# A decay factor fetched as one row and spread by matmuls, in place of a broadcast transfer

## The chip, the cores and the metric

The kernel runs on one core of a Trainium2 chip. The metric is the device time of one execution in microseconds (us); lower is better. A core has five engines with queues of their own: TensorE (PE, matmuls and, beside them, weight loads), VectorE (DVE), ScalarE (ACT), GpSimd (POOL) and SyncE (SP, which here only issues DMAs). ACT and POOL issue DMAs too. Each engine executes its queue in the written order, and a waiting instruction holds those behind it.

## The reference

Two layers. The first is an attention with exponential decay, over 4 batches, 8 heads, 768 positions and 64 channels, in blocks of 64 positions with a running state; each head h has its own decay lam[h], a number between 0.97 and 0.99. The second multiplies each token's 512 values by w_in (512 x 2048), applies a piecewise quadratic activation, and multiplies by w_out (2048 x 512).

```python
Dmask = np.where(rel >= 0, lam[:, None, None] ** rel[None, :, :], 0.0)
lam_pow = lam[:, None, None] ** (pos[None, :, None] + 1)
lam_block = lam ** block
...
intra = np.einsum('bhic,bhjc->bhij', qb, kb) * Dmask[None]
intra = np.einsum('bhij,bhjd->bhid', intra, vb)
inter = np.einsum('bhid,bhde->bhie', qb * lam_pow[None], kv_state)
out[:, :, sl] = intra + inter
...
h = x @ w_in
mid = ~neg & ~pos
g = np.where(pos, h, np.where(neg, 0.0, (h + beta) ** 2 / (4.0 * beta)))
return (g @ w_out).astype(np.float32)
```

lam is an input of 8 float32 numbers, 32 bytes.

## The kernel before, in words

The decay between two positions i and j is lam to the power i - j. The kernel writes it as a product: q at position i is multiplied by lam to the i and k at position j by lam to the minus j, with positions counted from the middle of the sequence. These factors stand in tables, one value for each position (partition) and head. `tables` (L110) makes a pair of them: DVE multiplies the positions by ln lam (`arg`, L113), and ACT takes the exponential twice, `tk` for k (L115) and `tq` for q (L117). The pair `tke`/`tqe` (argument `arge`) serves the first four units of work, the pair `tkd`/`tqd` (`argd`) all others. For this every partition needs ln lam of all 8 heads: L93 fetches lam into all 128 partitions of `lam_b` by a DMA that ACT issues, and ACT takes the logarithm, `ln_lam` (L104).

The first 512 tokens are computed in four units, u = 0 to 3, each with 256 positions and 4 heads. A unit loads q, k and v (`x0f`, `x1f`, `x2f`, L302, three DMAs of 256 KB on SP's queue). `qs` (POOL) and `ks` (DVE, both L315) multiply by the tables, `vs` (L313) casts v. PE transposes qs and ks (L329); ACT, and for later units DVE, copy the result from PSUM to `qT` and `kT` (L336). PE then makes the scores (`ps`, L373), which DVE masks (`sc`, L381), the state update (`pu`, L349, copied by ACT to `ue`, L364), and the two output terms (`py`, L393 and L408), which ACT copies to `xT` (L419). The remaining tokens follow in chunks of 128. The second layer takes 512 tokens at a time: L606 multiplies by w_in, ACT and DVE apply the activation, L639 multiplies by w_out. Its weights come in pieces by DMAs on POOL's queue (L152, L153); the first waits for the third unit's k load.

The order on each engine is written out by a planner, `run_plan`: every operation has a guessed duration, its needs and a due time, and the planner simulates the engines and emits the instructions in the order that this gives. The plan begins at 5000 ns for the engines; what stands before (constants, lam, tables) is emitted first, in program order. Between PE's first operations the planner puts warm-up matmuls on a tile of zeros `zz` (`warm`, L272 to L275), 4 x 128 columns or 128 columns each, into one PSUM bank, `ph`. How many is decided by the nominal time `at`, which starts at the first number of `WARM`:

```python
        at, n1 = WARM[0], 0
        for t, _, x in sorted(out_seq, key=lambda p: p[:2]):
            if x.eng == "PE" and n1 < 2:
                while at < t - (200 if at < WARM[1] else WARM[2]):
                    one_ns = 58 if at > WARM[1] else 110
                    n = 4 if at + 4 * one_ns < t - 200 else 1
                    warm(n)
                    at += n * one_ns
```

PSUM tiles named `po` come from a pool of one buffer; the transposes of the first unit's ks write there.

Of the kernel before, what the change touches and what calls it, by code (L numbers as in the profile page):

```python
# [8 lines left out]
F32 = mybir.dt.float32  # L9
BF16 = mybir.dt.bfloat16  # L10
I32 = mybir.dt.int32
AX = mybir.AluOpType
AF = mybir.ActivationFunctionType
# [10 lines left out]
def kernel(  # L24
# [16 lines left out]
    nc = tc.nc  # L41
    B, H, S, D = q.shape
# [8 lines left out]
    MS = 512  # L51
# [7 lines left out]
    RW, NR = 2, 3  # L59
    XT, MG, NQT, NQK, NVS, NUB, RING = 6, 6, 4, 4, 5, 4, 3.5  # L60
    DBG = False
    OB = 8

    const = ctx.enter_context(tc.tile_pool(name="const", bufs=1))
# [10 lines left out]
    rp = ctx.enter_context(tc.tile_pool(name="rp", bufs=NR))  # L75
    op = ctx.enter_context(tc.tile_pool(name="op", bufs=OB))
    PS = bass.MemoryType.PSUM
    pp_h = ctx.enter_context(tc.tile_pool(name="pp_h", bufs=2, space=PS))
# [3 lines left out]
    pp_o = ctx.enter_context(tc.tile_pool(name="pp_o", bufs=1, space=PS))  # L82
# [6 lines left out]
    SYNC = mybir.DependencyInfo(mybir.DependencyClass.Sync, mybir.DependencyReason.DATA)  # L89

    nc.scalar.preload_act_table_set("natural_log_exp_and_others")
    lam_b = const.tile([128, H], F32)
    nc.scalar.dma_start(out=lam_b, in_=lam.partition_broadcast(128))  # L93


    NE = 4
# [3 lines left out]
    make_identity(nc, ident)  # L100
    zz = const.tile([128, MS], BF16)
    nc.vector.memset(zz, 0.0)
    ln_lam = const.tile([128, H], F32)
    nc.scalar.activation(out=ln_lam, in_=lam_b, func=AF.Ln)  # L104
    pos_e = const.tile([128, NE], F32)
    nc.vector.tensor_copy(pos_e, pos_ei.rearrange("p a b -> p (a b)"))
    one = const.tile([128, 1], F32)
    nc.vector.memset(one, 1.0)  # L108


    def tables(pos, n, name):
# [11 lines left out]
    for t, base in ((mask2, 0), (mask2b, 128)):  # L123
        nc.gpsimd.memset(t, 1.0)
        nc.gpsimd.affine_select(
            out=t, in_=t, compare_op=AX.is_ge, fill=0.0,
# [7 lines left out]
        out=causal, in_=causal, compare_op=AX.is_ge, fill=0.0,  # L134
# [34 lines left out]
    def add(key, eng, ns, fn, needs=(), due=None, extra=0, dma=0, perf=False, mode=("full", "full"), ring=1, slack=0, late=0):  # L169
        OPS[key] = Op(key, eng, ns, fn, list(needs), due, extra, dma, perf, mode, ring, slack)  # L170
        OPS[key].late = late
        ops.append(OPS[key])

    def run_plan(free):
# [42 lines left out]
        while len(out_seq) < len(ops):  # L217
# [33 lines left out]
            for u in users[x.key]:  # L251
                left[u.key] -= 1
                if left[u.key] == 0:
                    ready[u.eng].append(u)
# [8 lines that stand above are left out]
                at = t + x.ns  # L263
                n1 += x.key[0] == "l1"
            if DBG:
                print(f"{t / 1e3:9.3f} {min(x.due, 9e6) / 1e3:9.3f} {x.eng:5s} {x.ns:6.0f} {x.end / 1e3:9.3f} {x.key}")
            x.fn()

    WARM = (1400, 7500, 700)
    wbank = []  # L270

    def warm(n):  # L272
        if not wbank:
            wbank.append(pp_h.tile([128, MS], F32, name="ph", tag="ph"))
        nc.tensor.matmul(wbank[0][:, 0:128 * n], lhsT=zz[:, 0:128], rhs=zz[:, 0:128 * n], start=True, stop=True, skip_group_check=True)  # L275

    def mm(*cols):
        return sum(c / 2.4 + 3 for c in cols)

# [372 lines left out]
    def f_ylast(part):  # L652
        cs = slice(CUT, d_model) if part else slice(0, CUT)
        if part == 0:
            osb["last"] = op.tile([128, d_model], F32, name="osb", tag="osb")
        nc.scalar.copy(out=osb["last"][:, cs], in_=py_t["last", part][:, cs])

    def f_stlast(part):
        cs = slice(CUT, d_model) if part else slice(0, CUT)
        nc.sync.dma_start(out=out[n_tok - 128:n_tok, cs], in_=osb["last"][:, cs])  # L660

    def f_y(s, ms):
        osb[s, ms] = op.tile([128, d_model], F32, name="osb", tag="osb")
        nc.scalar.copy(out=osb[s, ms], in_=py_t[s, ms])  # L664

    def f_out(s, ms):
        m0 = s * MS + ms * 128
        if s == 0:

            for j in range(2):  # L670
                nc.gpsimd.dma_start(out=out[m0:m0 + 128, :].rearrange("(p j) n -> j p n", j=2)[j], in_=osb[s, ms][HD[j], :])
        elif s < NST - 1:
            nc.gpsimd.dma_start(out=out[m0:m0 + 128, :], in_=osb[s, ms])  # L673
        else:
            nc.sync.dma_start(out=out[m0:m0 + 128, :], in_=osb[s, ms])
# [160 lines left out]
    for n1, (_, s, i, p) in enumerate(l1_order):  # L836
        prev = bank[on_y[n1]]
        n = PARTS.get(s, 1)
# [18 lines left out]
    for n2, (_, s, ms, kg) in enumerate(l2_order):  # L857
        n = PARTS.get(s, 1)
# [5 lines left out]
        if y == NCH - 1:  # L864
            if kg == 0:
                for part, n in ((0, CUT), (1, d_model - CUT)):
# [3 lines left out]
                    add(("y", y + part), "ACT", 400 - 240 * part, lambda part=part: f_ylast(part),  # L870
                        [("last", part), ("y", y - 1 + part), ("st", y - OB)], extra=95)
                    add(("st", y + part), "SP", 550 if s else 1100, lambda part=part: f_stlast(part), [("y", y + part), ("st", y - 1 + part)], due=-1,
# [5 lines left out]
        if kg == 3:  # L878
            add(("y", y), "ACT", 490, lambda a=(s, ms): f_y(*a), [("l2", n2), ("y", y - 1), ("st", y - OB)], extra=95)
            add(("st", y), "POOL" if s < NST - 1 else "SP", 1600 if s == 0 else 800 if s < NST - 1 else 550, lambda a=(s, ms): f_out(*a),  # L880
# [34 lines left out]
```

## Time and profile before

| | us |
|---|---|
| median of 3 runs | 209.01 (208.78 to 209.41) |
| the profiled execution, whole | 210.35 |
| its span, first to last instruction | 208.6 |
| PE busy in the span | 201.6 |
| DVE busy | 140.0 |
| ACT busy | 120.4 |
| issue of lam's transfer (L93) | 0.83 |
| start of `ln_lam` (L104) | 4.94 |
| start of the first `qs` on POOL (L315) | 5.84 |
| PE's warm-up matmuls before the first transposes | 15, from 1.26 to 6.56 |

The profile is of one execution; times in it count from the span's start. Busy time of PE is the time in which matmuls are under way, not that at which it is at its peak. An engine's idle time is put down to whatever released it last. Instructions that issue a DMA stand as SPq, ACTq or POOLq, with the time that the issue took.

### The profile page before, as it was taken

Reading aid. Unit: us, or ns where it says so; the run is one execution under the profiler, and the core shown is the slowest. Engines: PE = TensorE matmul, PEld = TensorE weight load, DVE = VectorE, ACT = ScalarE, POOL = GpSimd, SP = SyncE. Lnnn points to the kernel's source line nnn. Section 1 sums busy time; section 2 is a strip of 40 time slices with the busy share of each in tenths; the row PEclk is TensorE's granted clock in tenths of the full one; section 3 lists DMA queues with packets and bytes.
Section 4 is the critical chain, followed back from the end, with each engine's and each line's share of the span. In section 5 each row is a group of like instructions: output and inputs, shape, how many; then the busy total and the mean of one; then the engine's idle time right before and its main releaser. Section 6 shows DMA issues by size and latency. Waiting matters only on the chain.

```text
span 208.6 us, 6389 instructions
## 1 busy us (share of the span) xinstructions
PE 201.6 (97%) x2754; PEld 137.1 (66%) x2754; DVE 140.0 (67%) x245; ACT 120.4 (58%) x225; POOL 72.8 (35%) x95
## 2 busy tenths in 40 slices
PE   7779999999999999999999999999999999999994
PEld 2457887446866876666766767667667666666643
DVE  0575697453898786998877989976866656354510
ACT  2564675225865767585675786575675565464421
POOL 5598200145255173763554354335511011010000
PEclk9996999999999999999999999999999999999999
DMA  4999999999999999999999999999822002011112
GB/s 106 296 246 177 201 202 199 234 214 179 173 232 211 196 235 222 212 246 228 173 199 280 170 257 219 205 177 213 147 50 104 3 5 98 0 50 53 50 50 101
DMA packets 95051, 34.49 MB, mean 165 GB/s; under 512 B 82352, under 2 KB 93360, under 8 KB 95024
## 3 DMA queue, kind: packets, MB, share of 16 engines
q1 hardware_dynamic: 88464, 24.65, 65.4%
q0 software_dynamic: 6416, 9.44, 21.2%
q8 instruction: 21, 0.34, 0.7%
q14 instruction: 6, 0.05, 0.1%
q10 hardware_dynamic: 144, 0.00, 0.0%
HBM read 27.27 MB, written 6.29 MB: 161 GB/s over the span
## 4 chain that ended last, share of the span: by engine, by line
PE 90%; SPq 4%; DMA 3%; ACT 1%; issue 1%; DVE 0%; ACTq 0%
PE ph L606 40%; PE py L639 39%; SPq L302 4%; DMA x1f<-in_k_dram 3%; PE py L649 2%; PE ps L500 1%; PE py L606 1%; PE ps L492 1%; PE pu L527 1%; PE po L527 1%; PE po L511 1%; PE py L408 1%; DVE ks L315 0%; PE pu L511 0%; PE py L393 0%
## 5 line engine op out<-in xcount | busy, mean ns | idle before, releaser
L606 PE MATMUL ph<-xT,w_in_sb 128*128 128x256 bf16 (+1 forms) x872 | 94.8, 258 | 0.0
L639 PE MATMUL py<-w_out_sb,gT 128*128 128x512 bf16 x368 | 91.1, 379 | 0.0
L614 ACT ACTIVATE r<-ph,one 128x512 bf16<-128x512 f32 x93 | 63.9, 687 | 46.5 <-PE ph L606 40.9
L606 PEld LDWEIGHTS <-w_in_sb 128*128 128x128 bf16 x896 | 76.7, 98 | 19.9 <-issue 0.2
L639 PEld LDWEIGHTS <-gT 128*128 128x128 bf16 x368 | 34.9, 98 | 28.4
L622 DVE TENSOR_SCALAR t<-r 128x1024 bf16<-128x1024 bf16 x48 | 24.9, 518 | 32.3 <-ACT r L614 32.1
L630 DVE TENSOR_TENSOR gT<-w,t 128x1024 bf16<-128x1024 bf16 x48 | 39.8, 830 | 1.4
L625 DVE TENSOR_TENSOR w<-r,t 128x1024 bf16<-128x1024 bf16 x48 | 36.9, 769 | 1.6
L453 POOL TENSOR_TENSOR kq<-x1f,tkd 128x512 bf16<-128x512 f32 x18 | 20.5, 1139 | 23.8 <-DMA x1f<-in_k_dram 21.7
L673 POOL DMA_DIRECT2D out_dram<-osb x16 | 9.1, 571 | 50.1 <-ACT osb L664 48.4
L453 POOL TENSOR_TENSOR kq<-x0f,tqd 128x512 bf16<-128x512 f32 x18 | 20.6, 1144 | 15.6 <-DMA x0f<-in_q_dram 15.4
L664 ACT COPY osb<-py 128x512 f32<-128x512 f32 x23 | 13.5, 587 | 12.1 <-PE py L639 11.4
L565 DVE TENSOR_TENSOR sd<-ps,diag 128x256 bf16<-128x256 f32 x36 | 13.5, 415 | 3.0 <-PE ps L500 3.0
L443 ACT CAST vs<-x2f 128x512 bf16<-128x512 f32 x20 | 12.3, 616 | 2.2 <-DMA x2f<-in_v_dram 2.2
L539 DVE TENSOR_TENSOR st<-st,ps 128x256 f32<-128x256 f32 x30 | 12.4, 414 | 0.5
L544 ACT CAST us<-st 128x512 bf16<-128x512 f32 (+1 forms) x18 | 10.5, 581 | 2.0 <-DVE st L539 1.8
L548 ACT CAST xT<-po 128x256 bf16<-128x256 f32 x18 | 6.8, 377 | 4.7 <-PE pu L511 4.1
L450 POOL TENSOR_TENSOR kq<-x0f,tqd 128x512 bf16<-128x512 f32 x2 | 2.1, 1040 | 20.1 <-DMA x0f<-in_q_dram 20.1
L548 ACT CAST xT<-pu 128x256 bf16<-128x256 f32 x18 | 6.7, 374 | 2.3 <-PE po L511 2.3
L527 PEld LDWEIGHTS <-vs 64*64 64x64 bf16 x288 | 3.7, 107 | 6.5 <-issue 5.9
L275 PE MATMUL ph<-zz 128*128 128x512 bf16 (+1 forms) x18 | 6.3, 510 | 1.3 <-DVE one L108 1.3
L381 DVE TENSOR_TENSOR sc<-ps,mask 128x512 bf16<-128x512 f32 x8 | 5.2, 681 | 2.4 <-PE ps L373 2.4
(89 smaller groups left out, 135.3 us busy)
## 6 DMA issues: line engine op xcount, KB each, us to landing
x0f<-in_q_dram SPq DMA_DIRECT2D x24, 256.0 KB, 5.6
x1f<-in_k_dram SPq DMA_DIRECT2D x24, 256.0 KB, 5.2
x2f<-in_v_dram SPq DMA_DIRECT2D x24, 256.0 KB, 5.5
out_dram<-osb POOLq DMA_DIRECT2D x16, 256.0 KB, 4.0
w_out_sb<-in_moe_w_out_dram POOLq DMA_DIRECT2D x4, 512.0 KB, 13.6
w_in_sb<-in_moe_w_in_dram POOLq DMA_DIRECT2D x3, 512.0 KB, 7.0
out_dram<-osb POOLq DMA_DIRECT2D x8, 128.0 KB, 4.4
out_dram<-osb SPq DMA_DIRECT2D x3, 256.0 KB, 2.0
```

The lines of the kernel that those rows point to most:

```text
L443: (nc.scalar.copy if eng is nc.scalar else eng.tensor_copy)(t, qkv_ld[c, x])
L453: eng.tensor_tensor(t.rearrange("p (i g) d -> p g i d", g=2), qkv_ld[c, x].rearrange(h4, g=2), tb.rearrange(h4, g=2), op=AX.mult)
L539: nc.vector.tensor_tensor(st[c][:, a], st[c][:, 0] if a else st[c - 1][:, 1], kv[c][a], op=AX.add)
L548: nc.scalar.copy(out=get_xT(s)[:, :, off:off + 64], in_=po_of(c, a))
L565: nc.vector.tensor_tensor(sc_sb[c][:, par], pst[c, par], _bc(diag, 1, HP), op=AX.mult)
L606: nc.tensor.matmul(ph[:, j * m:(j + 1) * m], lhsT=w_in_sb[:, ko, (ni + j) * 128:(ni + j + 1) * 128], rhs=xT[s][:, ko, part * m:(part + 1) ...
L614: nc.scalar.activation(out=r_t[grp][:, i, :], in_=ph_t[s, ni, part], func=AF.Relu, bias=one[:, 0:1])
L622: nc.vector.tensor_scalar(t_t[grp], r, 0.5, 1.0, op0=AX.mult, op1=AX.min)
L625: nc.vector.tensor_tensor(w_t[grp], r, t_t[grp], op=AX.subtract)
L630: nc.vector.tensor_tensor(gT[s][:, f - RW * n:f, part * m:(part + 1) * m], w_t[grp].rearrange("p a (b m) -> p (a b) m", m=m), t_t[grp].rea ...
L639: nc.tensor.matmul(py_t[s, ms], lhsT=gT[s][:, ko, ms * 128:(ms + 1) * 128], rhs=w_out_sb[:, ko, :], start=(ko == 0), stop=(ko == FO - 1))
L664: nc.scalar.copy(out=osb[s, ms], in_=py_t[s, ms])
```

## The change

lam is fetched into one partition (`lam_1`, 1 x 8 float32). Three bfloat16 numbers are split off it in turn, each the rounded rest of what the ones before left (three casts and two subtractions on DVE, on one partition), and each is multiplied on PE by a column of ones: a matmul with `ones` (1 x 128) as weights adds up the three parts in float32 on all 128 partitions of a PSUM tile `po`. ACT takes the logarithm from there. Five warm-up matmuls are emitted ahead of the three, and the planner's nominal time for warm-ups starts by 5 x 440 ns later. The definition of `warm` moves up unchanged.

```diff
+    WARM_LAM = 5
...
-    lam_b = const.tile([128, H], F32)
-    nc.scalar.dma_start(out=lam_b, in_=lam.partition_broadcast(128))
+    lam_1 = const.tile([1, H], F32)
+    nc.scalar.dma_start(out=lam_1, in_=lam.rearrange("(o h) -> o h", o=1))
...
-    ln_lam = const.tile([128, H], F32)
-    nc.scalar.activation(out=ln_lam, in_=lam_b, func=AF.Ln)
...
+    ones = const.tile([1, 128], BF16)
+    nc.vector.memset(ones, 1.0)
...
+    for _ in range(WARM_LAM):
+        warm(4)
+    lam_p = [const.tile([1, H], BF16, name=f"lam{i}") for i in range(3)]
+    lam_r = [const.tile([1, H], F32, name=f"lamr{i}") for i in range(2)]
+    lam_b = pp_o.tile([128, MS], F32, name="po", tag="po")[:, 0:H]
+    rest = lam_1
+    for i in range(3):
+        nc.vector.tensor_copy(lam_p[i], rest)
+        if i < 2:
+            nc.vector.tensor_tensor(lam_r[i], rest, lam_p[i], op=AX.subtract)
+            rest = lam_r[i]
+        nc.tensor.matmul(lam_b, lhsT=ones, rhs=lam_p[i], start=(i == 0), stop=(i == 2))
+    ln_lam = const.tile([128, H], F32)
+    nc.scalar.activation(out=ln_lam, in_=lam_b, func=AF.Ln)
...
-    WARM = (1400, 7500, 700)
+    WARM = (1400 + 440 * WARM_LAM, 7500, 700)
```

On PE's queue this puts three matmuls of 8 columns behind the first five warm-ups; the ten others, and all that follows on every engine, keep their order. On DVE the five small operations stand behind the constants and ahead of `arge`.

More of the change, by code (lines that the diff above doesn't have):

```diff
@@ L108, with warm @@
     nc.vector.memset(one, 1.0)
+    ones = const.tile([1, 128], BF16)
+    nc.vector.memset(ones, 1.0)
+    wbank = []
+    def warm(n):
+        if not wbank:
+            wbank.append(pp_h.tile([128, MS], F32, name="ph", tag="ph"))
+        nc.tensor.matmul(wbank[0][:, 0:128 * n], lhsT=zz[:, 0:128], rhs=zz[:, 0:128 * n], start=True, stop=True, skip_group_check=True)
+    for _ in range(WARM_LAM):
[12 more added lines that the diff above has]
+    nc.scalar.activation(out=ln_lam, in_=lam_b, func=AF.Ln)
     def tables(pos, n, name):
@@ L267, in run_plan @@
             x.fn()
-    WARM = (1400, 7500, 700)
[L270 to L275, printed above, removed]
+    WARM = (1400 + 440 * WARM_LAM, 7500, 700)
     def mm(*cols):
```

## The prediction

> **What bounds the kernel now.** I read the page's chain that ended last first: it tells who is worth speeding up.
>
> ```profile
> PE 201.6 (97%) x2754; PEld 137.1 (66%) x2754; DVE 140.0 (67%) x245; ACT 120.4 (58%) x225; POOL 72.8 (35%) x95
> PE 90%; SPq 4%; DMA 3%; ACT 1%; issue 1%; DVE 0%; ACTq 0%
> ```
>
> PE is nine tenths of the chain, so the body isn't touched by an edit to the start. What can move is the moment at which PE's own run begins. The chain in order of time, cut to the first 30 us, shows that moment:
>
> ```profile
> 2.98 1.86 SPq L302
> ...
> 9.33 5.27 DMA x1f<-in_k_dram
> 14.60 0.02 issue
> 14.62 1.01 DVE ks L315
> 15.63 0.05 issue
> 15.67 0.40 PE po L329 x4
> ```
>
> (Start, length.) Up to 14.6 us the chain is the twelve loads of the first four units on SP's queue; the eleventh, k of the last unit, releases DVE, and from 15.67 it is PE. No lam stands in it. Where lam stands, the timelines of ACT, POOL and DVE say (start, length, in brackets the idle time before and its releaser):
>
> ```profile
> 0.83 0.42 ACTq L93 DMA_DIRECT2D lam_b<-in_lam_dram  x1
> 4.94 0.21 ACT L104 ACTIVATE ln_lam<-lam_b 128x8 f32<-128x8 f32 x1 [2.86 <-DMA lam_b<-in_lam_dram]
> 5.84 1.04 POOL L315 TENSOR_TENSOR qs<-x0f,tqe 128x512 bf16<-128x512 f32 x1 [1.60 <-ACT tqe L117]
> 6.67 0.76 DVE L315 TENSOR_TENSOR ks<-x1f,tke 128x512 bf16<-128x512 f32 x1 [0.97 <-DMA x1f<-in_k_dram]
> 9.01 0.69 DVE L381 TENSOR_TENSOR sc<-ps,mask 128x512 bf16<-128x512 f32 x1 [1.58 <-PE ps L373]
> 11.99 0.73 DVE L315 TENSOR_TENSOR ks<-x1f,tke 128x512 bf16<-128x512 f32 x1 [0.76 <-DMA x1f<-in_k_dram]
> 14.62 1.00 DVE L315 TENSOR_TENSOR ks<-x1f,tke 128x512 bf16<-128x512 f32 x1 [0.37 <-DMA x1f<-in_k_dram]
> ```
>
> lam lands 4.1 us after its issue and holds only the first qs, and that by little: x0f, issued at 0.81 with a landing after 4.9, is there at 5.7, so an instant lam alone would give 0.1 us. From 9.01 DVE works without a stop except for two waits for loads, 0.76 and 0.37.
>
> The table by stretches of time shows how the loads begin (last three numbers: clock, DMA share, GB/s):
>
> ```profile
> 2.00:2.50 0.50, 0.50 (x2) 0.15 (x1) 0.00 (x0) 0.09 (x1) 0.50 (x2) 1.00 0.08 12
> 2.50:3.00 0.50, 0.50 (x3) 0.21 (x2) 0.00 (x0) 0.00 (x0) 0.43 (x2) 1.00 0.40 92
> 3.00:3.50 0.50, 0.50 (x3) 0.22 (x2) 0.00 (x0) 0.00 (x0) 0.44 (x2) 1.00 0.72 134
> 3.50:4.00 0.50, 0.50 (x3) 0.17 (x2) 0.00 (x0) 0.00 (x0) 0.35 (x4) 1.00 0.68 177
> 4.00:4.50 0.50, 0.50 (x2) 0.15 (x1) 0.00 (x0) 0.00 (x0) 0.24 (x1) 1.00 0.80 238
> 4.50:5.00 0.50, 0.50 (x2) 0.15 (x1) 0.00 (x0) 0.06 (x1) 0.00 (x0) 1.00 1.09 320
> ```
>
> The rate climbs for 2.5 us and is full just when lam lands at 4.9. By the queues' view lam is 144 packets (128 rows of 32 bytes and 16 that signal) on the same 16 engines; in the packet records they are spread evenly from 1.9 to 4.6 us, one every 20 ns.
>
> **The change, part by part.**
>
> *Removed: the broadcast's packets.* 128 rows become one. What the loads gain, G, is shown nowhere. Lowest: 0, if the climb is the loads' own; fewer packets can't slow them. Highest: the whole climb, 2.5 us less the time that its bytes take at 320 GB/s: (12+92+134+177+238) x 0.5 / 320 = 1.02, so 1.48 us. I take 1.2: the climb ends with lam's landing, and the four engines whose lam signals come first (3.1 us) also have x0f first (3.8 against 5.7 for the last); 0.25 I leave as the loads' own start.
>
> *The row's landing, L.* Not earlier than 0.83 + 1.9 = 2.7, the shortest issue-to-landing of the page (an output store of 192 KB late in the run); not later than 4.9, as the broadcast. I take 2.75, being 32 bytes at a time when little flows. [...]
>
> *Added on the lam path.* Five dependent small DVE operations: from the start of the cast of pos (5.29) to its reader argd (5.49) it is 0.20 a step, so 4 x 0.20 + 0.12 (cast of pos_e) = 0.92; ends 0.6 (five times 0.12) and 1.35 (five of 0.21 and 0.06 of wait). Then 0.06 to PE (ks ends 7.43, PE starts 7.49), a matmul of 8 columns 0.25 (a 64-column one takes 0.2, the first cold ones of 512 0.6), 0.03 to ACT. So Ln starts 1.3 after the landing, not 0.02: at 4.05 in place of 4.94. From Ln to qs stays 0.90, so qs could start at 4.95 and ks too, if x0f and x1f are there (5.7 and 6.6, less G: 4.5 and 5.4). Behind the waiting cast on DVE stand only arge and argd, which need ln_lam anyway; the memset of ones (0.06) and the removal of Ln's direct wait cost nothing there.
>
> *Moved on PE.* Five of the fifteen warm-up matmuls now stand ahead of the lam matmuls, ten behind; their number and all that follows is in the old order. PE spaces the 512-column ones by 0.427 us, so the five end at 1.26 + 5 x 0.427 = 3.4; the third lam matmul can start at 2.75 + 0.05 + 0.92 + 0.06 = 3.8, a hole of 0.4. Then 6 x 0.427 + 4 x 0.107 = 2.99, to 6.85. The first transposes of qs start at 6.94 now. So the first unit doesn't start earlier, however soon lam is: queued behind the ten, it stands at 6.9. Call the delay of this point d; here 0. ACT's Ln reads PSUM, bank po, long before kT's transposes need it (7.49).
>
> *What is late next.* With the first unit fixed, sc stays at 9.01, and DVE then runs in its written order. Loads earlier by 1.2 are there at 10.8 and 13.4; DVE is free for the third ks at 11.23 (end of kT) and, 2.26 busy later (now 11.99 to 14.25, the end of the next kT), for the fourth at 13.50. So both waits go and the rest is DVE-bound: 14.62 - 13.50 = 1.12. POOL follows: its third qs, load at 9.9, ends at 10.9, the two weight issues (1.72) end at about 12.6, qs of the last unit then 12.6 against 13.98. The weights wait for the x1f load of the third unit, so they come 1.2 earlier as well. From 15.67 PE is the chain, and a start earlier by s ends it earlier by s. In short: shift of the end = the larger of -G and d - 1.13.
>
> **Sum.** Load gain 1.2, cut to 1.1 by DVE; first unit 0; PE lam matmuls hidden before 6.9. The profiled execution is 210.35 (span 208.6 and 1.75 around it), 1.34 over the median of the runs; the difference belongs to the start, so I take it off both: 210.35 to 209.25, and 209.01 to 207.9.
>
> **The rivals.**
>
> *The climb is not lam's (G = 0).* For: any queue has a start, and SP's fifth issue stands for 1.86 us from 2.98, as if its queue were full. Against: the even spread of lam's packets over just this time. DVE still waits for the same loads, and if L is 2.7 to 3.6 then d, 0 to 0.8, vanishes in the 1.13 of slack: 208.9 to 209.1.
>
> *PE stands still for lam.* The row lands no sooner than the broadcast, at 4.9: the third lam matmul comes at 5.95, the ten warm-ups end at 8.95, d = 2.0, and 0.9 stays: 209.9. With a hole from 3.4 to 5.95 PE also may not be at full clock when the transposes come. The spacing shows its clock: 0.427 for 512 columns up to 6.2, 0.056 for 128 at 7.0, after 5.3 us of unbroken warm-up. If it stays slow until 10.0, the unit's transposes and scores take about twice 0.4 + 0.4, some 0.3 on the path: 210.3. It decides from L = 4.05 (d = 1.13), and is measurable from 4.7. For: four engines' signals lie beyond 4.5 now. Against: those engines had eight rows each. [...]
>
> *The half clock falls away.* From 16.8 to 20.2 the granted clock is 0.50:
>
> ```profile
> 17.00:18.00 1.00, 1.00 (x39) 0.95 (x36) 0.23 (x2) 0.51 (x2) 1.00 (x2) 0.50 1.33 185
> ```
>
> Eight L606 matmuls take 1.82 there and 0.87 later; L408 0.87 against 0.42; L373 0.73 against 0.42: 1.7 in all. If the denser start keeps the clock up: 206.2. Against: the start is only 1.1 denser.
>
> *The gain is given back* at a later weight or load wait: 208.8 to 209.2; against it, PE has nearly no idle time after 18 us.
>
> **Chances.** Forecast 0.45 (own range 207.3 to 208.4: G from 0.6 to 1.48, d to 0.3); the clock kept up 0.10; climb not lam's 0.20; PE standing 0.17; given back 0.08. A measurement tells 0.3%, 0.63 us, from no change. Faster: 0.45 + 0.10 and a little of the rest, 0.56; same: 0.25, the third and fifth less that, plus PE standing briefly; slower 0.19. Range 206.6 to 209.8: it leaves out most of the kept clock and of PE standing.
>
> **What would show it.** lam_1 landing before 3.2 and the rate of 320 GB/s before 3.5 us; ln_lam near 4; first qs transposes still near 6.9; the third and fourth ks without a DMA wait, the fourth at 13.5. Wrong if the GB/s climb is unchanged, if PE waits past 5 us for lam, or if the half clock moves.

## The result, and the profile after

| | before | after |
|---|---|---|
| median | 209.05 us (13 runs, 208.78 to 210.22) | 208.35 us (13 runs, 207.75 to 209.56) |
| ratio of the runs | | 0.9964, 95% interval 0.9947 to 0.9981 |
| profiled execution, its span | 210.35, 208.6 | 207.96, 206.3 |

The change saves 0.70 us at the medians; the interval, times 209.05, is 0.40 to 1.11 us. The forecast was 207.9; the measured median is 0.45 above it and lies just inside the range of the forecast itself (207.3 to 208.4).

The page of after, its busy times, its broadcast queue and its chain that ended last:

```profile
PE 196.4 (95%) x2725; PEld 135.8 (66%) x2757; DVE 136.8 (66%) x251; ACT 120.4 (58%) x225; POOL 73.5 (36%) x95
q10 hardware_dynamic: 2, 0.00, 0.0%
PE 90%; SPq 3%; DMA 3%; issue 2%; DVE 0%; ACT 0%
```

The 144 packets of lam have become 2: one row and one that signals. PE is still nine tenths of the chain. PE's busy time can't be set against that of before to a microsecond: 32 of after's matmuls are missing among the records (2725 against 2757 weight loads), and before's own first profile has a stretch at half clock, shown below.

The chain's early part in after (start, length, what):

```profile
2.96 0.51 SPq L317
...
8.33 5.30 DMA x1f<-in_k_dram
13.63 0.02 issue
13.65 0.98 DVE ks L330
14.64 0.05 issue
14.68 0.40 PE po L344 x4
```

It is the chain of before, link by link: SP's issues, the eleventh load, the fourth ks, PE. From the eleventh load on it is earlier by 0.97 to 1.00 (9.33 to 8.33, 14.62 to 13.65, 15.67 to 14.68). So the limit in this stage is the same one, only sooner.

The two profiled executions differ by 2.39, more than twice that. Before was therefore profiled a second time. The table by stretches of this second execution, and of after, at the place where the first one of before had a granted clock of 0.50 (length, PE, PEld, DVE, ACT, POOL, clock, DMA share, GB/s):

```profile
17.00:18.00 1.00, 1.00 (x41) 0.79 (x40) 0.49 (x3) 0.55 (x3) 1.00 (x2) 1.00 1.28 167
```

```profile
17.00:18.00 1.00, 1.00 (x23) 0.74 (x21) 0.95 (x2) 0.35 (x2) 1.00 (x2) 1.00 1.23 188
```

Both ran at full clock. The second execution of before took 209.21 with a span of 207.48. Its first q load, expected complete at 5.4 to 5.8, was so at 5.90, its fourth ks, expected at 14.4 to 14.8, stood at 14.90, and its span had been expected near 207.3. From its fourth ks to ACT's first activation of L606's result it took 4.07, the first one 5.33: 1.26 of the first one's excess is its half clock, which most executions of the kernel before do not have (in 40 of its 66 timed runs on three chips the granted clock is 0.997 or more over the span). Against the second execution after is 1.22 shorter in span, and 1.25 earlier at the fourth ks: the whole gain stands at the start and nothing is given back behind it.

The first microseconds of after, timelines of ACT, DVE, PE and POOL (start, length; in brackets the idle time before and its releaser):

```profile
0.83 0.52 ACTq L94 DMA_DIRECT2D lam<-in_lam_dram  x1
2.04 0.54 DVE L124 CAST lam<-lam 1x8 bf16<-1x8 f32 x1 [0.67 <-DMA lam<-in_lam_dram]
...
3.50 0.27 PE L128 MATMUL po<-lam,ones 1*128 1x8 bf16 x3
3.81 0.18 ACT L130 ACTIVATE ln_lam<-po 128x8 f32<-128x8 f32 x1 [1.73 <-PE po L128]
4.77 1.57 POOL L330 TENSOR_TENSOR qs<-x0f,tqe 128x512 bf16<-128x512 f32 x1 [0.51 <-ACT tqe L139]
6.40 0.40 PE L344 MATMUL ph<-ident,qs 128*128 128x128 bf16 x4 [0.74 <-POOL qs L330]
8.41 0.69 DVE L396 TENSOR_TENSOR sc<-ps,mask 128x512 bf16<-128x512 f32 x1 [2.97 <-PE ps L388]
11.00 0.73 DVE L330 TENSOR_TENSOR ks<-x1f,tke 128x512 bf16<-128x512 f32 x1 [0.37 <-DMA x1f<-in_k_dram]
13.65 0.97 DVE L330 TENSOR_TENSOR ks<-x1f,tke 128x512 bf16<-128x512 f32 x1 [0.40 <-DMA x1f<-in_k_dram]
```

The row is there 1.2 us after its issue, and the logarithm starts at 3.81 instead of 4.94. The first qs waits for the table tqe, as in before: there tqe ended 0.1 us after x0f was complete (5.75 and 5.66), here 0.9 us (4.68 and 3.76). The third and fourth ks still wait for their loads.

The table by stretches of after, last number GB/s:

```profile
2.00:2.50 0.50, 0.50 (x2) 0.15 (x1) 0.46 (x1) 0.09 (x1) 0.50 (x2) 1.00 0.51 106
2.50:3.00 0.50, 0.50 (x3) 0.15 (x1) 0.43 (x3) 0.00 (x0) 0.43 (x2) 1.00 1.02 304
3.00:3.50 0.50, 0.50 (x2) 0.00 (x0) 0.43 (x3) 0.00 (x0) 0.44 (x2) 1.00 1.13 335
3.50:4.00 0.50, 0.50 (x5) 0.28 (x5) 0.06 (x1) 0.18 (x1) 0.35 (x4) 1.00 1.14 340
4.00:4.50 0.50, 0.50 (x3) 0.24 (x2) 0.45 (x3) 0.16 (x2) 0.26 (x1) 1.00 1.07 275
4.50:5.00 0.50, 0.50 (x4) 0.20 (x3) 0.38 (x2) 0.50 (x4) 0.23 (x1) 1.00 1.13 263
5.00:5.50 0.50, 0.50 (x7) 0.31 (x4) 0.44 (x1) 0.04 (x1) 0.50 (x1) 1.00 0.87 211
```

The climb to 300 GB/s, 2.5 us long before, takes half a microsecond. Added up to 5.0 us, after has moved 816 KB and before 486: 330 KB, at 320 GB/s 1.03 us. A dip from 4 to 6 us, which before does not have, brings the lead down to 231 KB at 6.0; by 9.0 it is 299 again. At 10.0 us the lead is 2258 - 1971 = 287 KB, at the 292 GB/s of that stretch 0.98 us: the 0.97 of the fourth ks.

### The profile page after: what moved, and what is told of

Read it like the earlier page. It is cut to its first block, busy times and chain, and to the rows that moved or that the text cites. A ratio compares the mean times of both kernels' runs of the same rounds, so it can differ in the third digit from the quotient of the medians.

```text
span 206.3 us, 6368 instructions
## 1 busy us (share of the span) xinstructions
PE 196.4 (95%) x2725; PEld 135.8 (66%) x2757; DVE 136.8 (66%) x251; ACT 120.4 (58%) x225; POOL 73.5 (36%) x95
## 4 chain that ended last, share of the span: by engine, by line
PE 90%; SPq 3%; DMA 3%; issue 2%; DVE 0%; ACT 0%
PE ph L621 41%; PE py L654 38%; SPq L317 3%; DMA x1f<-in_k_dram 3%; PE py L664 2%; PE ps L515 1%; PE py L621 1%; PE ps L507 1%; PE pu L542 1%; PE po L542 1%; PE po L526 1%; PE py L423 1%; DVE ks L330 0%; PE pu L526 0%; PE ps L571 0%
## 5 line engine op out<-in xcount | busy, mean ns | idle before, releaser
L654 PE MATMUL py<-w_out_sb,gT 128*128 128x512 bf16 x338 | 86.0, 379 | 2.3 <-issue 1.1
L637 DVE TENSOR_SCALAR t<-r 128x1024 bf16<-128x1024 bf16 x48 | 23.2, 483 | 35.9 <-ACT r L629 35.4
L645 DVE TENSOR_TENSOR gT<-w,t 128x1024 bf16<-128x1024 bf16 x48 | 38.3, 797 | 1.4
L640 DVE TENSOR_TENSOR w<-r,t 128x1024 bf16<-128x1024 bf16 x48 | 35.4, 737 | 1.6
L515 PE MATMUL ps<-vs,kq 64*64 64x64 bf16 x264 | 6.2, 196 | 0.0
## 6 DMA issues: line engine op xcount, KB each, us to landing
w_out_sb<-in_moe_w_out_dram POOLq DMA_DIRECT2D x4, 512.0 KB, 14.8
```

Source lines behind the costliest of these rows:

```text
L637: nc.vector.tensor_scalar(t_t[grp], r, 0.5, 1.0, op0=AX.mult, op1=AX.min)
L640: nc.vector.tensor_tensor(w_t[grp], r, t_t[grp], op=AX.subtract)
L645: nc.vector.tensor_tensor(gT[s][:, f - RW * n:f, part * m:(part + 1) * m], w_t[grp].rearrange("p a (b m) -> p (a b) m", m=m), t_t[grp].rea ...
L654: nc.tensor.matmul(py_t[s, ms], lhsT=gT[s][:, ko, ms * 128:(ms + 1) * 128], rhs=w_out_sb[:, ko, :], start=(ko == 0), stop=(ko == FO - 1))
```

## The experiments

Three theories were to be told apart. The first: the 128 rows of the broadcast held the loads back, and the gain is the loads'. The rivals: the gain comes from the earlier tables (ln_lam, 1.13 earlier), or from PE's new start, and the loads' climb is their own. In the diffs, "+" stands against the changed kernel unless another is named. All ratios are against the kernel before, timed on the same chip (medians there 208.81 to 209.04).

**The broadcast put back, unread** (e1). The tables still come from the row; the broadcast only uses the DMA engines.

```diff
     nc.scalar.dma_start(out=lam_1, in_=lam.rearrange("(o h) -> o h", o=1))
+    junk = const.tile([128, H], F32)
+    nc.scalar.dma_start(out=junk, in_=lam.partition_broadcast(128))
```

> The changed kernel, with the old broadcast transfer of lam issued again right behind the one-row fetch, into a tile that nothing reads. Theory P (the broadcast's 128 small packets hold the loads back, and the gain is the loads'): the first q load is complete only at 5.0 to 5.8 us instead of 3.8, the eleventh load at 14.2 to 14.8 instead of 13.6, and the time is that of the kernel before, ratio 0.998 to 1.002. Rival T (the gain is that the tables are ready sooner): ln_lam stays near 3.8 us and the ratio stays 0.995 to 0.998. Rival C (the gain is a matter of the clock at the start, the warm-up being split): ratio as T.

209.37 us, ratio 1.0021 (1.0007 to 1.0036): the gain is gone. The table by stretches of e1:

```profile
3.00:3.50 0.50, 0.50 (x2) 0.00 (x0) 0.43 (x3) 0.00 (x0) 0.44 (x2) 1.00 0.69 159
3.50:4.00 0.50, 0.50 (x5) 0.28 (x5) 0.06 (x1) 0.18 (x1) 0.35 (x4) 1.00 0.51 149
4.00:4.50 0.50, 0.50 (x2) 0.15 (x1) 0.45 (x3) 0.16 (x2) 0.26 (x1) 1.00 1.02 148
4.50:5.00 0.50, 0.50 (x3) 0.19 (x2) 0.13 (x1) 0.50 (x4) 0.23 (x1) 1.00 0.71 187
```

The broadcast now stands second on ACT's queue, so its rows run from 2.94 to 4.93 us. Ahead of it the rate is that of after (290 against 304); while its rows run, it is about half of after's from 3.0 to 4.5 (149 against 340) and 0.7 of it at the end, although the engines are busy for 50 to 100% of their time. x0f was already through at 3.77, x1f came at 6.39 in place of 4.65, the fourth ks at 14.44, though ln_lam stood at 3.81 as in after. Early tables and PE's new start, both of which e1 has, give nothing while the broadcast runs. e1 is even slower than before by 0.2%; its chain goes through a weight load, issued by POOL at 14.83 and awaited until 22.49, which those of before do not. So e1's loss against after (1.0 at the medians, 1.2 by the ratios) is only in part the later fourth ks (0.79); the wait for the weights was not followed further.

**128 rows from 128 places, unread** (e2), and **32 rows of the broadcast, unread** (e6).

```diff
+    junk = const.tile([128, H], F32)
+    nc.scalar.dma_start(out=junk, in_=q[0, 0, 0:128, 0:H])
```

```diff
+    junk = const.tile([32, H], F32)
+    nc.scalar.dma_start(out=junk, in_=lam.partition_broadcast(32))
```

> As the run with the unread broadcast, but the 128 rows of 32 bytes come from 128 different places (the first 8 channels of 128 positions of q), so that only the source of the rows differs. If small packets as such hold the loads back: first q load complete at 5.0 to 5.8 us, as with the broadcast. If it is that all rows read the same 32 bytes: first q load complete at 3.8 to 4.2 us and the ratio to before 0.995 to 0.998.

> As the run with the unread broadcast of lam, but to 32 partitions in place of 128. If each further read of the same 32 bytes costs a fixed time (some 20 ns, as the packets of the kernel before are spaced), the hold is a quarter: the first k load complete at 4.9 to 5.3 us, between 4.7 without and 6.4 with 128 rows, the eleventh load 0.2 to 0.4 later than without. If it is a fixed price of any repeated source: as with 128 rows.

e2: 208.29 us, ratio 0.9969 (0.9952 to 0.9986), the time of the change. The table by stretches of e2:

```profile
3.00:3.50 0.50, 0.50 (x2) 0.00 (x0) 0.43 (x3) 0.00 (x0) 0.44 (x2) 1.00 1.13 302
3.50:4.00 0.50, 0.50 (x5) 0.28 (x5) 0.06 (x1) 0.18 (x1) 0.35 (x4) 1.00 1.12 335
4.00:4.50 0.50, 0.50 (x2) 0.15 (x1) 0.45 (x3) 0.17 (x2) 0.26 (x1) 1.00 1.18 286
```

Nothing is held while the rows run. By the packet records the 128 rows of 32 bytes went from 2.91 to 3.39, 0.48 us, where e1's, equal in number, size and queue, took 1.99. What differs is the source: in e1 all rows read the same 32 bytes. So neither the packets' number nor their smallness alone is what cost time in before; what is left is that they all want one place. The two runs also differ in the tensor that is read (lam or q); 128 reads of one row of q were not run.

The fourth ks of e2 starts at 13.30, 0.35 earlier than in after, and yet the time is the same. The chain of its profile does not go through that ks but through POOL's queue to a load of w_out that ends at 29.12 and for which PE waits 0.2:

```profile
16.39 12.73 DMA w_out_sb<-in_moe_w_out_dram
```

e6: 208.46 us, ratio 0.9964 (0.9938 to 0.9989). Its 32 rows took 0.43 us (2.93 to 3.36), about e1's time per row; but x1f came at 4.66, where a quarter of the hold was expected (4.9 to 5.3). While they ran, the rate was that of after (302 and 331 GB/s). One stretch falls to 139 at 4.0, after they had ended; after, e3 and e5 have dips there too (211, 194, 207 at the lowest), and whether this deeper one is the rows' is open. The time shows no hold.

**No lam at all** (e3, an edit of the kernel before; the decay is computed from a constant).

```diff
-    nc.scalar.dma_start(out=lam_b, in_=lam.partition_broadcast(128))
+    nc.vector.memset(lam_b, 0.98)
```

> The kernel before, with lam not fetched at all: lam_b is set to 0.98 by a memset, so the decay is that of a constant. No transfer, no small matmuls; tables ready near 2.3 us. Theory P: the loads run as in the changed kernel (first q load 3.7 to 4.0, eleventh 13.2 to 13.8) and the ratio to before is that of the change, 0.994 to 0.998, since the tables are not what the end waits for. Rival T: with the tables 2.5 us sooner than in the changed kernel the ratio falls below 0.993.

208.29 us, ratio 0.9964 (0.9951 to 0.9978), although the tables are ready at 2.9 us here and PE has neither lam matmuls nor split warm-ups. The row, five small DVE operations and three matmuls cost nothing that can be measured, and a lam that is there at once would win nothing more.

**A shorter way for lam** (e5): no split, one float32 matmul.

```diff
-    ones = const.tile([1, 128], BF16)
+    ones = const.tile([1, 128], F32)
...
+    nc.tensor.matmul(lam_b, lhsT=ones, rhs=lam_1, start=True, stop=True)
```

> The changed kernel with lam spread by one float32 matmul of the row itself in place of three bfloat16 ones, so without the five VectorE operations: ln_lam at 2.9 to 3.4 us in place of 3.8. If the end waits for the loads, as the run without any lam says: ratio to before 0.995 to 0.998, as the change. If the split still stands on the path: below 0.995.

208.38 us, ratio 0.9966 (0.9939 to 0.9993): the time of the change. The expected earlier logarithm missed. Timelines of PE and ACT of e5:

```profile
3.50 0.59 PE L120 MATMUL po<-lam,ones 1*128 1x8 f32 x2
4.13 0.18 ACT L122 ACTIVATE ln_lam<-po 128x8 f32<-128x8 f32 x1 [2.04 <-PE po L120]
```

The matmul stood behind the five warm-ups until 3.50, as in after, and then took 0.59 in two parts, where the three bf16 ones take 0.27. The split costs DVE 1.52 us, and these were hidden under PE's warm-ups.

**lam late.** Eight dependent copies of the row on DVE ahead of the split: in e4 as it is, in e7 with ten warm-ups ahead of the lam matmuls and five behind, in e10 with ten ahead and ten behind.

```diff
+    lam_d = [const.tile([1, H], F32, name=f"lamd{i}") for i in range(8)]
     rest = lam_1
+    for t in lam_d:
+        nc.vector.tensor_copy(t, rest)
+        rest = t
```

```diff
-    WARM_LAM = 5
+    WARM_LAM = 10
...
-    WARM = (1400 + 440 * WARM_LAM, 7500, 700)
+    WARM = (1400 + 440 * 5, 7500, 700)
```

(The last two lines in e10 only.)

> The changed kernel with eight more dependent copies of the row on VectorE before the split, so that the small matmuls come about 2.2 us later (8 x 0.28), near 5.8 us, with ten warm-ups behind them; loads as in the changed kernel. By the rule of the prediction (shift = the larger of the load gain and the delay of the first transposes less VectorE's slack) the first transposes start at 7.8 to 8.9 instead of 6.4, the slack left beside the loads is 0.8, and the time rises by 0.6 to 1.6 us over the changed kernel: ratio to before 0.999 to 1.004. If the lam path lies off the path to the end altogether: ratio 0.995 to 0.998.

> The run with eight more dependent copies, but with ten warm-ups ahead of the small matmuls in place of five, so that PE has no hole while it waits and fewer warm-ups stand behind. If the loss of that run (1.5 us over the changed kernel) comes of the hole and of what is queued behind it (warm-ups, and the clock released only at 10.6 us): clock released by 7.2 us, first transposes at 7.5 to 7.9 in place of 8.2, and most of the loss gone, ratio to before 0.997 to 1.0005. If it comes of the late tables alone: ratio 1.002 to 1.005 as there.

> The run with eight more dependent copies, with ten warm-ups ahead of the small matmuls and the full ten behind, so that PE is busy without a hole from 1.3 to about 7.6 us and the tables alone are late. If late tables are the small part of the loss of 1.5 us and the clock is the large one: granted clock 1.0 in most runs, first transposes near 7.8, fourth ks at 14.2 to 14.9 and the ratio to before 0.998 to 1.001. If late tables alone cost it: ratio 1.003 or more.

| | ln_lam | PE without work | half clock | first transposes | fourth ks | time | ratio |
|---|---|---|---|---|---|---|---|
| after | 3.81 | | until 4.27 | 6.40 | 13.65 | 208.35 | 0.9964 |
| e4 | 5.32 | 3.6 to 5.2 | until 10.63 | 8.18 | 15.84 | 209.83 | 1.0040 (1.0025 to 1.0054) |
| e7 | 5.51 | 6.0 to 7.85 | 8.16 to 18.4 | 7.85 | 15.75 | 210.33 | 1.0057 (1.0037 to 1.0078) |
| e10 | 5.92 | 7.5 to 8.27 | 12.68 to 16.09 | 8.27 | 15.69 | 210.08 | 1.0064 (1.0039 to 1.0088) |

All three are slower than before: this is the rival in which PE stands for lam, made to happen. e7 missed what was expected of it: with fewer warm-ups behind the lam matmuls PE stood idle from 6.0 to 7.85, and at 8.16 the clock fell; all ten runs have a granted clock under 0.997. Two stretches of e7:

```profile
7.00:8.00 1.00, 0.15 (x3) 0.15 (x4) 0.00 (x0) 0.00 (x0) 1.00 (x2) 1.00 1.22 306
...
9.00:10.00 1.00, 0.67 (x27) 0.58 (x25) 0.00 (x0) 0.54 (x2) 0.95 (x2) 0.50 1.21 304
```

The seventh number from the left is the clock: 1.00 while PE is 15% busy, 0.50 two microseconds later, with PE at work again. In e7 the granted clock went to 1.00 at 4.75, fell to 0.50 at 8.16, 3.41 us later, and was back at 18.4, 10.24 us after the fall; of the 3.41 us PE was idle for 1.86. Idle time of about that length does not always go with a fall: in the second execution of before the clock went to 1.00 at 3.93, PE was idle from 5.33 to 7.15, 1.82 us, and the clock stayed at 1.00. How much idle time is enough, these runs don't show.

e10's hole is 0.77 us, about that of after (0.74), and yet it is as slow, as the rival in its expectation had it. Timelines of PE and DVE of e10:

```profile
8.27 0.40 PE L348 MATMUL ph<-ident,qs 128*128 128x128 bf16 x4 [0.77 <-POOL qs L334]
...
10.89 1.07 DVE L334 TENSOR_TENSOR ks<-x1f,tke 128x512 bf16<-128x512 f32 x1
...
12.82 0.68 DVE L334 TENSOR_TENSOR ks<-x1f,tke 128x512 bf16<-128x512 f32 x1
...
15.35 0.42 DVE L355 COPY kT<-po 128x512 bf16<-128x512 bf16 x1 [0.42 <-PE po L348]
15.69 0.68 DVE L334 TENSOR_TENSOR ks<-x1f,tke 128x512 bf16<-128x512 f32 x1
```

No ks waits for a load. Against after, ln_lam is 2.11 later, the first transposes 1.87, the third ks 1.82, the fourth 2.04: late tables cost nearly their whole delay. Since the clock also dropped in most of e10's runs (0.984 to 0.992 over the span), its time alone doesn't separate the two. The third ks does, as the drop begins only at 12.68; ahead of the fourth, DVE waits 0.42 for transposes that run at half clock (14.70, 0.61 long), so a part of its delay is the clock's.

**The loads on two queues** (e9). After's dip from 4 to 6 us falls together with SP's issues of 1.01 and 1.30 us at 4.11 and 5.17. v of the first two units goes to ACT's queue, behind the row.

```diff
+    v_ld = {}
+    for u in range(2):
+        t = ld.tile([128, H // 2, 2 * D], F32, name="x2f", tag="x2f")
+        d = nc.scalar.dma_start(out=t, in_=v[0, 4 * u:4 * u + 4, ...
+        v_ld[u] = (t, d)
...
+        if x == 2 and u in v_ld:
+            qkv_ld["e", u, x], ld_dma["e", u, x] = v_ld[u]
+            return
```

> The changed kernel with the v loads of the first two units issued on ScalarE's queue, right behind the row, in place of SP's. The loads of the changed kernel gain 1.9 us at the first and only 1.0 at the eleventh; their rate falls from 340 to 211 GB/s between 4 and 5.5 us while SP's issues take 1.0 and 1.3 us. If that dip comes of the one queue: no dip, eleventh load below 13.2, the two DVE waits for k loads gone, ratio 0.990 to 0.994. If it lies in the reads themselves: dip as before, eleventh load 13.3 to 13.9, ratio 0.994 to 0.999.

207.75 us (4 runs), ratio 0.9942 (0.9926 to 0.9959), just short of what was expected. It has the lowest median of all kernels run, below after's by 0.6, of which 0.24 is the chip (before's median there is 208.81, not 209.05); the intervals overlap. The table by stretches and the timeline of DVE of e9:

```profile
4.00:4.50 0.50, 0.50 (x2) 0.15 (x1) 0.44 (x3) 0.15 (x2) 0.27 (x1) 1.00 1.16 344
4.50:5.00 0.50, 0.50 (x3) 0.18 (x2) 0.14 (x1) 0.50 (x4) 0.22 (x1) 1.00 1.18 308
5.00:5.50 0.50, 0.50 (x3) 0.21 (x2) 0.04 (x1) 0.05 (x1) 0.50 (x1) 1.00 1.19 284
```

```profile
13.41 0.94 DVE L338 TENSOR_TENSOR ks<-x1f,tke 128x512 bf16<-128x512 f32 x1 [0.43 <-DMA x1f<-in_k_dram]
```

The dip is gone, so it comes with the single queue. It was worth little: by 13.0 us e9 has moved some 40 KB more than after, at 292 GB/s 0.14 us, and the fourth ks is 0.24 earlier. Of DVE's two waits for k loads, which had been expected to go, that of the fourth ks stays, 0.43. The gain is small, but it comes with a higher rate of the transfers: 284 to 344 GB/s from 4.0 to 5.5 us, where in after the rate fell from 275 to 211 while SP's issues took 1.01 and 1.30. Whether the long issues are the cause of that fall or go along with it is not shown; in e9 an issue of 2.15 us on SP, at 5.79, stands beside 284 to 289 GB/s.

All profiles without a delayed lam in one table: bytes moved by 10.0 us, added up from the tables by stretches, and the start of the fourth ks.

| held by a broadcast | KB | ks | not held | KB | ks |
|---|---|---|---|---|---|
| before | 1971 | 14.62 | after | 2258 | 13.65 |
| before, again | 1894 | 14.90 | e2 | 2245 | 13.30 |
| e1 | 2007 | 14.44 | e3 | 2183 | 14.22 |
| | | | e5 | 2196 | 14.05 |
| | | | e6 | 2205 | 13.64 |
| | | | e9 (two queues) | 2273 | 13.41 |

No kernel of the one group reaches the other, in either column. Without e9 the means of the fourth ks are 14.65 and 13.77, 0.88 apart: within the interval of the measured gain (0.40 to 1.11). Leaving out e1 and e2 too, whose chains go through weight loads, they are 14.76 and 13.89, 0.87 apart. Kernels of one group also differ among themselves by up to 0.9 us in single profiles, which is why the start of one profile can't give the gain to better than some tenths.

## Why the prediction was right, point by point

*What bounds the start: right.* The eleventh load, the fourth ks, then PE; a shift there arrives at the end in full (0.97 at the fourth ks and 1.00 at PE's transposes; against the repeat of before 1.25 and 1.22 in the span). It need not go on so: in e2 a fourth ks that is another 0.35 earlier gave nothing. The chain there goes through a load of weights instead, though PE's wait for it, 0.2, is less than what was lost.

*The mechanism of G: right, its size a little large.* That the climb was lam's and not the loads' own, which had stood as a rival at 0.20, is shown from three sides: taken away by another way (e3) the gain stays, put back (e1) it goes, and with the rows' places apart (e2) it stays. The forecast took 1.2 of at most 1.48, and its sum 1.1. The bytes give 1.03 at 5.0 us and 0.98 at 10.0, the fourth ks 0.97; against the repeat of before 1.25. At the first load alone the gain was 1.90 (complete at 3.76 instead of 5.66), beyond the bound: the bound was made of bytes, and x0f was complete with the last of its sixteen signals, which were spread over 1.9 us before and over 0.3 us after. That surplus is not worth anything further on. The term that was mis-sized is thus G at the loads that count: 1.2 taken, 1.1 of it in the sum, 0.97 measured in the profile, 0.70 in the runs' medians; this is nearly all of the 0.45 between 207.9 and 208.35.

*What held them: wrongly put.* The prediction spoke of 128 rows and 144 packets, as if their number were the load. (Nor was their spread quite even: half of the rows had gone by 2.97, of 1.94 to 4.57.) e2 shows that as many rows from different places hold nothing, and e6 that 32 rows from one place hold nothing that can be seen.

*L and the way of lam: two errors that cancelled.* The row landed at 2.01, 1.18 after the start of its issue and below the lower bound of 2.7, which came from an output store of 192 KB that took 1.9. The split took 1.52 (2.04 to 3.56) instead of 0.92, for the first cast took 0.54 and the others 0.28 and 0.26 instead of 0.20. ln_lam was forecast at 4.05 and came at 3.81.

*"The first unit doesn't start earlier": wrong, without consequence.* The transposes were put at 6.9 behind ten warm-ups at 0.427 each. Full clock came at 4.27 in this execution (6.59 and 3.93 in the two of before): the 512-column warm-ups start 0.427 apart ahead of it and 0.216 apart behind. The ten ended at 5.66, and the transposes, released by qs as in before, started at 6.40; sc moved from 9.01 to 8.41.

*"Both waits go and the rest is DVE-bound": wrong.* Both waits of ks stay, 0.37 and 0.40. DVE was 0.6 earlier and the load 0.2 later than forecast (13.63 against 13.4), so the loads and not DVE set the fourth ks. The two errors nearly meet, which is luck: 13.50 forecast, 13.65 measured.

*The slack of 1.13 for a late first unit: too kind.* By the rule "d - 1.13" e10, whose transposes stand 1.33 later than before's, would have lost 0.2 at the fourth ks. It lost 1.07 (15.69 against 14.62). A part of that is the half clock from 12.68 on: the 2.26 of DVE's work behind the third ks (12.82) would have put the fourth at an estimated 15.08, 0.46 late, and DVE's waits for PE behind the fall (0.14 and 0.42) make most of the rest. But 0.46 is still more than 0.2: the sum of DVE's busy times between sc and that ks was carried over from another profile, and in e10 the second ks took 1.07 instead of 0.68. The danger of the rival was underrated by this, but L was never near it.

*The half clock falls away: not the change.* It is absent in after, but also in the second execution of before. In the timed runs a granted clock under 0.997 is rarer in after (2 of 13) than in before (26 of 66), but the gain is there without it: the runs at 0.997 or more have a median of 208.22 in after and of 208.81 to 208.90 in before on its three chips. Taking its cost off both sides, as the forecast did by going to the median, was right. The price of this rival, 206.2, was not: it takes 1.7 more off a median whose runs mostly have no half clock to lose, and in the profile the half clock cost 1.26.

*The gain is given back: not by the change.* From the fourth ks to the end of the span it is 192.61 us in after and 192.58 in the second execution of before. In e1 and e2, whose chains go through a weight load, it is 193.54 and 193.31.

Open are why two of SP's issues, at 4.11 and 5.17, take 1.0 and 1.3 us when the loads run free, why e6's 32 rows do not hold the loads while they run and e1's 128 do, and what the remaining 0.2 to 0.3 between the shift in the profile (0.97) and in the medians (0.70) is made of; the spread of the fourth ks from execution to execution is large enough for it, but that it is the cause was not shown.

## What to carry to other kernels

A broadcast from one small place in memory need not be free because it is small: here 128 rows, 4 KB, held the loads beside them to about half their rate for 1.5 us and to 0.7 of it for half a microsecond more (e1, 149 GB/s against after's 340 from 3.5 to 4.0), while beside 32 rows (e6) the rate was that of after (302 and 331 against 304 and 335, from 2.5 to 3.5); the broadcast's own reader in the kernel before would have gained an estimated 0.1 us from an instant lam (its table ended at 5.75, and x0f was complete at 5.66). Look at the rate of the other queues while it runs, and fetch one row and spread it on chip, if an engine has idle time just then. A gain in loads is worth what it is at the load on which the chain hangs (0.97 here), not at the first load (1.90), and only as long as the chain goes through that load: in e2 it went through the weights'.

## What was not expected of the hardware

- 128 rows of 32 bytes from one place took 1.99 us, from 128 places 0.48, on the same queue at the same time of the run; the other queue's rate was about 150 GB/s beside the one and about 300 beside the other.
- A transfer of a single row of 32 bytes was usable 1.2 us after the start of its issue (0.83 to 2.04).
- In after the first DVE operation on a 1x8 tile took 0.54 us and the next casts 0.28 and 0.26, the subtractions 0.15; in e7, from 4.18 on, each of the three casts took 0.16. The small operations of this chain were not of one price.
- A stretch in which PE did no work or only three tiny matmuls, 1.6 to 1.9 us long, among or behind the warm-ups was followed by up to 10 us of half clock (e4 until 10.63, e7 from 8.16 to 18.4). A hole of 1.82 us in the second execution of before was not, and in e10 the clock fell at 12.68 although the warm-ups had no hole and had kept PE busy until 7.5.
